# Convolution and channel mix on one core: casting loads, tap matrix from all partitions, a split first group, and the difference on VectorE

## The chip, the cores and the metric

One core of one Trainium2 chip runs the kernel. The metric is the device time of one execution in microseconds (us). A version has four runs in each comparison (the kernel before up to seven); I quote medians and, in brackets, the lowest and highest run.

## The reference

A causal convolution of seven taps runs along the sequence; its taps are a softmax, one set for each of eight heads of 24 channels. An RWKV channel mix follows.

```python
batch, seq, d_model, d_ff = (8, 4160, 192, 1024)      # 8 heads, 7 taps
w = softmax(weight)                                    # per head
x = conv(x, w)                                         # causal, per head
x_prev = shift(x, 1)                                   # one step back, zero first
xk = mu_k * x + (1.0 - mu_k) * x_prev                  # = x_prev + mu_k * (x - x_prev)
xr = mu_r * x + (1.0 - mu_r) * x_prev
k = np.maximum(xk @ w_k, 0.0)
v = k * k @ w_v
r = 1.0 / (1.0 + np.exp(-(xr @ w_r)))
return r * v
```

## The kernel before

Batches go in four pairs. A sequence is cut into blocks of 116 positions with a halo of 6, and nine blocks of both batches make a group. The convolution of one head and one group is one matmul against a banded matrix of that head's taps, the tile `toe`. The result is copied out of PSUM, transposed (`yT`), and mixed: `d = x - x_prev`, then `xk` and `xr`. The main loop has 260 slots, one for 128 of the 1024 hidden features and 512 positions of two batches. In a slot, TensorE makes `k` (4 matmuls), `r` (2) and `v` (8), ScalarE takes the relu, VectorE squares it. Convolutions and transposes of the next group are strewn into the slots.

The order is fixed by hand: each piece is put at a slot of its engine's table, and each engine executes in that order. These are the parts that the change touches:

```python
def cast_x(p, g, s):                       # GpSimd: float32 to bf16, head by head
    ...
    nc.gpsimd.tensor_copy(out=xbs[p, g][:, :, :, s, :],
                          in_=xf.rearrange("p n (h g) -> p h n g", h=H))
...
w_raw = const.tile([H, K], FP32)           # taps on 8 partitions
...                                        # softmax into w_row [8, 244]
w_scr = dram.tile([H, P, W], BF16)         # each row 128 times: 1024 pieces of 488 B
nc.sync.dma_start(out=w_scr, in_=w_row.unsqueeze(1).to_broadcast([H, P, W]))
toe = const.tile([P, H, BLK], BF16)        # read back one element further per partition
nc.sync.dma_start(out=toe, in_=bass.AP(tensor=w_scr.tensor, offset=w_scr.offset + K - 1,
                                       ap=[[W - 1, P], [P * W, H], [1, BLK]]))
...
def diff(p, s):
    ...
    nc.gpsimd.tensor_tensor(out=d[:, :, :L], in0=yT[:, :, c0 : c0 + L],
                            in1=yT[:, :, c0 - 1 : c0 - 1 + L], op=ALU.subtract)
...
nc.vector.tensor_tensor(out=o, in0=k_sb, in1=k_sb, op=ALU.mult)      # the square
```

## Time and profile before

The median is 548.74 us (546.62 to 548.99). I cut the trace by events on TensorE; times count from the start of the span. The span is what the trace shows of a run: 548.0 us of a run of 549.68.

| stretch of the kernel before | us | what rules it |
|---|---|---|
| start to the first k matmul | 44.11 | `toe` lands at 30.4, then convolution, transposes, difference, mixes |
| slots 0 to 15 | 32.44 | ScalarE's copies and the first mixes |
| slot 16 to the last matmul | 467.48 | TensorE, with stalls of 8.7 in all behind VectorE |
| last matmul to the end | 3.94 | last product and store |

To read it: TensorE is the bound wherever its slots repeat to the hundredth. So the question about any other engine is not how busy it is, but how often TensorE waits for it. Two more views put the same into one line each. First, the shares of the chain that ended last, by engine, on the page of the kernel before; then the longest early piece of that chain (start, length, what).

```profile
PE 68%; DVE 17%; issue 7%; DMA 6%; POOL 1%; ACT 1%; SPq 0%; DVEq 0%; POOLq 0%
```

```profile
7.95 14.67 DMA w_scr<-w_row
```

VectorE holds 17% of the chain, which would be 93 us: the share of a chain says who was followed, not what would be saved. One DMA of 488 KB takes 14.67 us of an opening of 44.

### The profile page before, as it was taken

Reading aid. Unit: us, or ns where it says so; the run is one execution under the profiler, and the core shown is the slowest. Engines: PE = TensorE matmul, PEld = TensorE weight load, DVE = VectorE, ACT = ScalarE, POOL = GpSimd, SP = SyncE. Lnnn points to the kernel's source line nnn. Section 1 sums busy time; section 2 is a strip of 40 time slices with the busy share of each in tenths; the row PEclk is TensorE's granted clock in tenths of the full one; section 3 lists DMA queues with packets and bytes.
Section 4 is the critical chain, followed back from the end, with each engine's and each line's share of the span. In section 5 each row is a group of like instructions: output and inputs, shape, how many; then the busy total and the mean of one; then the engine's idle time right before and its main releaser. Section 6 shows DMA issues by size and latency. Waiting matters only on the chain.

```text
span 548.0 us, 10694 instructions
## 1 busy us (share of the span) xinstructions
PE 498.3 (91%) x4248; PEld 359.5 (66%) x4248; DVE 488.6 (89%) x643; ACT 377.9 (69%) x539; POOL 172.7 (32%) x88
## 2 busy tenths in 40 slices
PE   0066889999999999999999999999999999999997
PEld 0032467777777677777777677777777677777776
DVE  1229999999999999999999999999999999989863
ACT  1044876878777686867777686867778587877772
POOL 4135513415034513515034522506134422204000
PEclk9999999999999999999999999999999999999999
DMA  7792013343432334343431334343341341111213
GB/s 199 188 267 65 2 53 114 108 124 108 138 110 60 112 112 123 105 128 109 125 121 49 114 121 123 94 138 109 122 120 49 109 123 61 49 58 45 73 60 95
DMA packets 77438, 57.28 MB, mean 105 GB/s; under 512 B 5778, under 2 KB 77132, under 8 KB 77388
## 3 DMA queue, kind: packets, MB, share of 16 engines
q1 hardware_dynamic: 75132, 54.57, 33.0%
q10 hardware_dynamic: 2256, 2.03, 1.3%
q8 instruction: 33, 0.54, 0.4%
q14 instruction: 17, 0.14, 0.1%
HBM read 30.53 MB, written 26.06 MB: 103 GB/s over the span
## 4 chain that ended last, share of the span: by engine, by line
PE 68%; DVE 17%; issue 7%; DMA 6%; POOL 1%; ACT 1%; SPq 0%; DVEq 0%; POOLq 0%
PE ps_v L390 25%; PE ps_k L314 15%; PE ps_k L310 15%; DVE k L355 7%; DVE xk L277 4%; PE ps_r L371 3%; PE ps_r L372 3%; PE ps_c L198 3%; DMA xf<-in_x_dram 3%; PE ps_t L229 3%; DMA w_scr<-w_row 3%; DVE o_sb L402 2%; DVE xr L277 2%; DVE yT L239 2%; ACT k_sb L341 1%
## 5 line engine op out<-in xcount | busy, mean ns | idle before, releaser
L341 ACT ACTIVATE k_sb<-ps_k 128x1024 bf16<-128x1024 f32 x260 | 265.9, 1023 | 120.7 <-PE ps_k L314 108.7
L355 DVE TENSOR_TENSOR k<-k_sb 128x1024 bf16<-128x1024 bf16 x256 | 254.5, 1005 | 5.6 <-ACT k_sb L341 5.1
L390 PE MATMUL ps_v<-wv,k 128*128 128x192 bf16 x2048 | 211.2, 246 | 3.8 <-DVE o_sb L402 2.7
L390 PEld LDWEIGHTS <-k 128*128 128x128 bf16 x2048 | 173.5, 98 | 39.9 <-issue 5.8
L255 POOL TENSOR_TENSOR d<-yT 128x1536 bf16<-128x1536 bf16 (+1 forms) x36 | 102.2, 2841 | 275.6 <-DVE yT L239 239.0
L310 PE MATMUL ps_k<-xk,wk 128*128 128x512 bf16 x512 | 153.6, 382 | 2.2 <-DVE xk L277 2.2
L314 PE MATMUL ps_k<-xk,wk 128*128 128x512 bf16 x512 | 153.6, 382 | 2.1 <-DVE xk L277 2.1
L314 PEld LDWEIGHTS <-wk 128*128 128x128 bf16 x512 | 50.4, 98 | 63.7 <-issue 4.0
L186 POOL CAST xb<-xf 128x1728 bf16<-128x1728 f32 x32 | 66.2, 2068 | 58.0 <-DMA xf<-in_x_dram 52.3
L402 DVE TENSOR_TENSOR o_sb<-ps_v,r_sb 128x384 f32<-128x384 f32 x132 | 71.8, 544 | 12.2 <-PE ps_v L390 10.3
L277 DVE SCALAR_TENSOR_TENSOR xr<-d,mu,yT 128x1024 bf16<-128x1024 bf16 x64 | 77.0, 1205 | 0.9
L198 PE MATMUL ps_c<-xb,toe 128*116 128x432 bf16 x128 | 46.6, 370 | 31.8 <-DMA toe<-w_scr 30.4
L277 DVE SCALAR_TENSOR_TENSOR xk<-d,mu,yT 128x1024 bf16<-128x1024 bf16 x64 | 69.8, 1092 | 2.9 <-POOL d L255 2.4
L380 ACT ACTIVATE r_sb<-ps_r 128x384 bf16<-128x384 f32 x132 | 65.1, 493 | 10.3 <-PE ps_r L372 8.2
L371 PE MATMUL ps_r<-wr,xr 128*128 128x192 bf16 x256 | 63.0, 246 | 3.3 <-DVE yT L239 3.2
L214 ACT CAST y<-ps_c 116x432 bf16<-116x432 f32 x96 | 44.9, 474 | 30.3 <-PE ps_c L198 30.3
L372 PE MATMUL ps_r<-wr,xr 128*128 128x192 bf16 x256 | 63.0, 246 | 0.0
L310 PEld LDWEIGHTS <-wk 128*128 128x128 bf16 x512 | 46.4, 98 | 4.3 <-issue 4.2
L198 PEld LDWEIGHTS <-toe 128*116 128x116 bf16 x128 | 17.6, 139 | 48.1 <-DMA toe<-w_scr 30.4
L229 PEld LDWEIGHTS <-y 116*128 116x128 bf16 x432 | 30.3, 100 | 23.2 <-issue 5.9
L239 DVE COPY yT<-ps_t 128x696 bf16<-128x696 bf16 (+1 forms) x80 | 38.4, 480 | 7.9 <-PE ps_t L229 7.0
L229 PE MATMUL ps_t<-ident,y 116*128 116x116 bf16 x432 | 36.2, 219 | 2.6 <-DVE yT L239 2.3
(46 smaller groups left out, 121.3 us busy)
## 6 DMA issues: line engine op xcount, KB each, us to landing
out_dram<-o_sb SPq DMA_DIRECT2D x128, 192.0 KB
xf<-in_x_dram SPq DMA_DIRECT2D x23, 864.0 KB
xf<-in_x_dram SPq DMA_DIRECT2D x9, 768.0 KB
stage<-in_moe_w_v_dram ACTq DMA_DIRECT2D x1, 768.0 KB
xf<-in_x_dram SPq DMA_DIRECT2D x8, 84.0 KB
stage<-in_moe_w_k_dram ACTq DMA_DIRECT2D x1, 512.0 KB
stage<-in_moe_w_k_dram ACTq DMA_DIRECT2D x2, 256.0 KB
w_scr<-w_row SPq DMA_DIRECT2D x1, 488.0 KB
```

Source lines behind the costliest of these rows:

```text
L198: nc.tensor.matmul(out=ps[:BLK].rearrange("p n s g -> p (n s g)"), lhsT=toe[:, h, :], rhs=xb[:, h, :, :, :].rearrange("p n s g -> p (n s g)"),
L229: nc.tensor.transpose(out=ps[:, c, i, :], in_=ys[p, g][:BLK, 2 * j + i, c * P : (c + 1) * P], identity=ident[:BLK, :BLK],)
L255: nc.gpsimd.tensor_tensor(out=d[:, :, :L], in0=yT[:, :, c0 : c0 + L], in1=yT[:, :, c0 - 1 : c0 - 1 + L], op=ALU.subtract,)
L277: nc.vector.scalar_tensor_tensor(out=o, in0=d[r0:r1, sl, :L], scalar=mu[r0:r1, i, part : part + 1], in1=yT[r0:r1, sl, c0 : c0 + L], op0=AL ...
L310: nc.tensor.matmul(out=ps[:, i, :], lhsT=wk[:, 0, fs], rhs=xk[:, i, :], start=True, stop=False)
L314: nc.tensor.matmul(out=ps[:, i, :], lhsT=wk[:, 1 + i, fs], rhs=xk[:, 2, :], start=False, stop=True)
L341: nc.scalar.activation(out=k_sb, in_=ps.rearrange("p a b -> p (a b)"), func=AF.Relu)
L355: nc.vector.tensor_tensor(out=o, in0=k_sb, in1=k_sb, op=ALU.mult)
L371: nc.tensor.matmul(out=o, lhsT=hi, rhs=wr[:, 0, :], start=True, stop=False)
L372: nc.tensor.matmul(out=o, lhsT=lo, rhs=wlo, start=False, stop=True)
L390: nc.tensor.matmul(out=o, lhsT=k2[:, f, t * P : (t + 1) * P], rhs=wv[:, f, :], start=(f == 0), stop=(f == NF - 1),)
L402: nc.vector.tensor_tensor(out=o_sb[:, :n, :], in0=v_ps.pop(m)[:, :n, :], in1=r_sbs.pop(m)[:, :n, :], op=ALU.mult)
```

## The change

The intent is to free VectorE of GpSimd's interference and to shorten the opening. x and the weights are loaded by GpSimd's DMAs, which convert to bf16 on the way, so the casts on GpSimd and VectorE and the float32 tiles go. The softmax of the taps is computed on all 128 partitions at once, so the scratch is written in 128 rows of 2 KB. The first group is split into 5 and 4 blocks, and its convolution outputs are copied by ScalarE and VectorE in turn. The difference moves from GpSimd to VectorE. Copies of weight pieces (`fill_tails`) are put on GpSimd at slot 4 in the table of loads. Three smaller moves come with it: `xb` gets three buffers in place of two, the loads of `mu` go from ScalarE's queue to SyncE's, and in the first pair the convolutions of the second and third groups and the differences and mixes that follow them get later slots. The diff, cut to its core:

```diff
-        xf = xfp.tile([P, GB, D], FP32, tag="xf")
-        nc.sync.dma_start(out=xf[:, lo:hi, :], in_=src)
-    def cast_x(p, g, s): ...
+    groups = [... [(0, 5, 0), (5, 4, 1)] + [(g * GB, GB, 2 * g) for g in range(1, NG)] ...]
+        xb = three.tile([P, GB, 2, D], BF16, tag="xb", name="xb")
+            nc.gpsimd.dma_start(out=xb[:, lo:hi, s, :], in_=...x...)      # casts
 ...
-    w_raw = const.tile([H, K], FP32)
+    w_raw = const.tile([P, H, K], FP32)
+    nc.scalar.preload_act_table(AF.Exp)
 ...
-    w_scr = dram.tile([H, P, W], BF16)
-    nc.sync.dma_start(out=w_scr, in_=w_row.unsqueeze(1).to_broadcast([H, P, W]))
+    w_scr = dram.tile([P, H, P], BF16)
+    nc.sync.dma_start(out=w_scr, in_=w_row)
-            ap=[[W - 1, P], [P * W, H], [1, BLK]],
+            ap=[[H * P - 1, P], [P, H], [1, BLK]],
+    nc.scalar.preload_act_table(AF.Sigmoid)
 ...
-        nc.vector.tensor_copy(out=w[:, 0, :], in_=wf[:, 0, :])            # and others
+        nc.gpsimd.dma_start(out=w[:, 0, :], in_=src[0:P, :])              # and others
+    def fill_tails():
+            nc.gpsimd.tensor_copy(out=w[0:LO, 3, :], in_=w[0:LO, 1, :])   # and one more
 ...
-            rhs=xb[:, h, :, :, :].rearrange("p n s g -> p (n s g)"),
+            rhs=xbs[p, g][:, :nb, :, h * G : (h + 1) * G],
 ...
-        nc.gpsimd.tensor_tensor(
+        nc.vector.tensor_tensor(
             out=d[:, :, :L],
 ...
+    at(early, -16, load_rest)
+    at(early, 4, fill_tails)
```

## The prediction

> **What bounds the kernel now.** I read the page's busy row first, then the slices, then the chain of waits in order of time, then the timeline of the first 80 us, then the groups.
>
> ```profile
> PE 498.3 (91%) x4248; PEld 359.5 (66%) x4248; DVE 488.6 (89%) x643; ACT 377.9 (69%) x539; POOL 172.7 (32%) x88
> ...
> PE   0066889999999999999999999999999999999997
> ...
> POOL 4135513415034513515034522506134422204000
> ...
> GB/s 199 188 267 65 2 53 114 108 124 108 138 110 60 112 112 123 105 128 109 125 121 49 114 121 123 94 138 109 122 120 49 109 123 61 49 58 45 73 60 95
> ```
>
> TensorE and VectorE are both near 90%, but they do not bound the same part. One slice is 13.7 us: TensorE does nothing in the first two, is part-filled in the next four, and is full from about 80 us to the end. The chain in that full part consists of TensorE pieces:
>
> ```profile
> 89.30 0.66 PE ps_v L390 x8
> ...
> 91.16 0.66 PE ps_v L390 x8
> ...
> 92.85 0.66 PE ps_v L390 x8
> ...
> 94.54 0.66 PE ps_v L390 x8
> ...
> 96.41 0.66 PE ps_v L390 x8
> ```
>
> The start-to-start distance is one slot of the schedule (there are 260): 1.69 us without extras (92.85 to 94.54), 1.87 with one convolution matmul, 2.00 with six transposes (87.31 to 89.30 in the same list). These repeat exactly wherever TensorE waits for nothing. Sixteen slots hold 8 convolutions and 27 transposes: 8 x 1.87 + 4 x 2.00 + 1.85 + 3 x 1.69 = 29.9 us. A pair of batches (64 such slots and a tail slot of 1.9) should take 121.4 us. The chain shows what it takes:
>
> ```profile
> 122.43 1.56 DVE k L355
> ...
> 246.42 1.56 DVE k L355
> ...
> 370.43 1.56 DVE k L355
> ```
>
> The same event comes back every 124.0 us, so VectorE costs about 2.7 us per pair. Summing actual minus best slot time over all slots from number 16 on, I get 9.2 us of stalls in the whole kernel. The rest is matmul floor. The opening is different:
>
> ```profile
> 7.95 0.84 SPq L116 DMA_DIRECT2D w_scr<-w_row  x1
> ...
> 30.40 0.97 PE L198 MATMUL ps_c<-xb,toe 128*116 128x432 bf16 x2 [30.40 <-DMA toe<-w_scr]
> ...
> 38.67 2.75 POOL L255 TENSOR_TENSOR d<-yT 128x1536 bf16<-128x1536 bf16 x1 [3.93 <-DVE yT L239]
> ...
> 41.45 5.76 DVE L277 SCALAR_TENSOR_TENSOR xk<-d,mu,yT 128x1024 bf16<-128x1024 bf16 x2 [2.42 <-POOL d L255]
> ...
> 44.11 1.01 PE L310 MATMUL ps_k<-xk,wk 128*128 128x512 bf16 x2 [2.19 <-DVE xk L277]
> ```
>
> The first convolution waits 30.4 us for the tap matrix (toe), the first k matmul starts at 44.1, and slot 16 starts at 76.55. The budget is therefore 44.1 (opening) + 32.4 (slots 0 to 15) + 467.5 (slot 16 to the last matmul at 544.0, of which 9.2 are stalls) + 4.0 (last store) = 548.0.
>
> The stalls come from this (the timeline, then the groups):
>
> ```profile
> 61.34 8.17 DVE L355 TENSOR_TENSOR k<-k_sb 128x1024 bf16<-128x1024 bf16 x3
> ```
>
> ```profile
> L355 DVE TENSOR_TENSOR k<-k_sb 128x1024 bf16<-128x1024 bf16 x256 | 254.5, 1005 | 5.6 <-ACT k_sb L341 5.1
> ...
> L255 POOL TENSOR_TENSOR d<-yT 128x1536 bf16<-128x1536 bf16 (+1 forms) x36 | 102.2, 2841 | 275.6 <-DVE yT L239 239.0
> ...
> L186 POOL CAST xb<-xf 128x1728 bf16<-128x1728 f32 x32 | 66.2, 2068 | 58.0 <-DMA xf<-in_x_dram 52.3
> ```
>
> Three squares take 8.17 us exactly while GpSimd runs a difference, a cast and a difference. Undisturbed, one takes 0.68 us (0.60 from start to start); the mean is 1.005.
>
> **What the Trainium skill says.** "SBUF — State Buffer", section "Who interferes with whom": a VectorE instruction with two SBUF inputs contends with a GpSimd instruction that reads SBUF, and the loser blocks for the whole instruction. The trace agrees (0.68 against 2.7 us for those three squares). "VectorE: DVE Perf Modes", section "The perf-mode tier table": tensor_tensor in bf16 reaches 2 elements per cycle. The square agrees: 1024/2/0.96 GHz = 533 ns plus some 150 fixed is 0.68. "Vector Engine (DVE) Microarchitecture Reference", section "Performance modes": 4-byte alignment makes no difference there. This matters as the difference reads one input at an odd column; no instruction of before tests it. "DMA: Bandwidth & Descriptors", section "SWDGE vs HWDGE vs iDMA": a casting DMA can only be issued by GpSimd, whose cores write every descriptor in software. The kernel before has no such DMA, so the trace gives no cost per descriptor. That is the largest unknown.
>
> **The change part by part.**
>
> 1. *GpSimd stops touching SBUF data* (32 casts, 66.2 us, and 36 differences, 102.2 us, go). VectorE gains 256 x (1.005 - 0.68) = 83 us on squares, and on the mixes 32 x (1.365 + 1.360 - 2 x 1.28) + 32 x (1.045 + 0.824 - 2 x 0.75) = 5 + 12 = 17 us. It takes on 36 differences at 1536/2/0.96 + 150 = 0.95 us, so 34 us. Its weight casts (some 5 us, opening only) go. Net busy time about 488 - 83 - 17 + 34 - 5 = 417 us. Per 16 slots, start to start: 16 x 0.60 + 8 x 0.47 + 4 x 0.45 + 0.27 + 4 x (1.19 + 0.66) + 2 x 0.87 = 24.6 us against TensorE's 29.9. VectorE gets slack, but time drops only by the stalls: at most 9.2 us, and I count 7.7 because transposes and mixes still bunch in some slots.
>
> 2. *Tap matrix.* The taps are computed on all partitions with the same small operations. The instruction order shows three table loads in a row before the exponential (the early load of the sigmoid table is placed ahead of it): 0.8 + 3 x 1.28 = 4.7 us, as early as the 5.1 of before, since ScalarE no longer issues DMAs. So w_row is ready near 6 us, as now. The scratch write then goes at once from 128 partitions in 2 KB pieces instead of 1024 pieces of 488 bytes that took 7.95 to 22.7 us: landing near 9. The tap read still has 1024 short pieces (7.3 us before, from 23.05 at the end of its issue to 30.39): landing near 15.
>
> 3. *First group of 5 blocks.* From first convolution to the first k matmul before: 13.7 us. After: convolution pieces of 240 columns evacuated by ScalarE and VectorE in turn, about 3 us; 15 transposes in place of 27, 4.0 x 15/27 = 2.2; difference 0.95 and mixes 1.28 + 0.75 without the contention that made them 2.75 + 5.76. That sums to about 8.5: 15 + 8.5 = 23.5. TensorE's order also has seven convolutions of the second group (4 blocks) ahead of the first k matmul, so they wait for the third batch of DMAs. I take 25, a gain of 19.
>
> 4. *Slots 0 to 15.* ScalarE has a 1.02 evacuation and a 0.51 convolution copy in each of the first ten: 15.3 us. Slots 10 to 15 carry convolutions and transposes together (1.69 + 0.31 + 0.18 = 2.18, three times, then 2.03 and 2 x 1.87): 12.3. With 2.4 for waits, 30.0 against 32.4.
>
> 5. *Casting loads.* Bytes moved are as before, less stage traffic; the stores stay. In the full part loads have two groups (60 us) of lead, so they hide. In the opening, blocks 9 to 17 are needed at slot 1. The bytes ahead of them and theirs (0.98 + 0.79 + 0.79 + 0.15 + 0.79 + 1.77 + 0.5 MB of taps = 5.8) need 22 us at the best rate of the slices, 267 GB/s: ready near 24 if bandwidth alone decides. I leave the 2.4 of part 4 for this.
>
> Sum: 25 + 30 + (467.5 - 7.7) + 4.0 = 518.8, so **519 us**.
>
> **The rivals.** *(a) Descriptor writing bounds the opening.* Some 6,100 row pieces must be described before blocks 9 to 17 are in (1268 + 256 + 1024 + 256 + 1024 + 2304 = 6132). At 2.5 ns each, with 1 us for each of 15 DMAs, that is near 30 us and costs a few us; at 5 ns it is 45 us, TensorE then stalls some 15 us at slot 1, and the time is near 533. At 10 ns it would be near 560, slower than before. For it: eight semaphores for these DMAs, each reused, tie the ninth DMA to the first. Against: the schedule of the first groups was evidently placed late to fit such loads. *(b) VectorE stays the bound.* If the difference runs at one element per cycle it takes 1.75 us; per 16 slots VectorE needs 26.2 of 29.9, so stalls of perhaps 3 to 5 us stay: 522. *(c) Convolution matmuls get slower*, because they now read runs of 24 columns rather than one run of 432. They lie on the bound: 0.18 us x 120; half as slow again is +11 us: 530. Nothing in the profile before shows such a read. *(d) The opening goes better* (first k matmul at 20, no wait at slot 1): 511.
>
> **Range and chances.** All but (a) and (c) keep the time between 511 and 525, and a mild (a) or (c) reaches 534. The verdict line for faster is 548.7 x 0.98 = 537.8, which needs a strong (a), or (a) and (c) together. I give 0.88 to faster, 0.09 to same, 0.03 to slower.
>
> **What would show it.** Right: toe lands near 15; first k matmul near 25; slot 16 near 55; squares at a mean below 0.75 us; the difference on VectorE at 0.95; the chain from 60 us on nearly all TensorE, a pair repeating every 121.5 us. Wrong: a convolution waiting for x in slots 1 to 10 (rival a); slots with a convolution longer than 1.87 (rival c); VectorE pieces in the chain of the full part (rival b); a load landing late after 100 us.

## More of the kernel before

The stalls are the sum, over all slots from 16 on, of a slot's time less the shortest of its kind (plain, with a convolution, with transposes). This count gives 8.7 us; the prediction has 9.2.

## The result

The changed kernel took 523.67 us (521.39 to 525.93) against 548.74. All outputs are right. The ratio is 0.955, with a 95% interval of 0.950 to 0.961. Ratios here are the mean time of one kernel's runs over that of the other's in the same rounds, so not quite the ratio of the medians. The predicted 519 is 4.7 us too low; the range of 509 to 534 held it. The profiled run took 521.39 us, one of the short ones.

Same cuts as before:

| stretch | before | after | change | predicted |
|---|---|---|---|---|
| start to the first k matmul | 44.11 | 26.25 | -17.9 | -19 |
| slots 0 to 15 | 32.44 | 30.01 | -2.4 | -2.4 |
| slot 16 to the last matmul | 467.48 | 459.07 | -8.4 | -7.7 |
| last matmul to the end | 3.94 | 4.34 | +0.4 | 0 |

The page of the changed kernel (busy row; slices of 13.0 us, in tenths; shares of the chain):

```profile
PE 492.5 (95%) x4256; PEld 360.1 (69%) x4256; DVE 425.3 (82%) x676; ACT 380.0 (73%) x545; POOL 51.9 (10%) x74
...
PE   0597999999999999999999999999999999999996
...
POOL 9532100001020000101002010100100000000000
...
PE 92%; DMA 3%; DVE 2%; ACT 2%; issue 0%; DVEq 0%; SPq 0%
```

VectorE fell from 89% to 82% and GpSimd's data work nearly vanished. The chain went from 68% to 92% TensorE: from slot 16 on, TensorE waits for almost nothing (stalls of 0.3 us in all by the same count, against 8.7; the view of TensorE's waits lists none between 57 and 512 us). The chain in order of time, one event per pair of batches, shows the period:

```profile
124.45 0.66 PE ps_v L388 x8
...
245.65 0.66 PE ps_v L388 x8
...
366.86 0.66 PE ps_v L388 x8
```

It is 121.2 us in place of 124.0. The groups of the page give the reason (mean ns of one instruction behind the busy us; L87 is the casting load, for which the time is that of issuing it):

```profile
L353 DVE TENSOR_TENSOR k<-k_sb 128x1024 bf16<-128x1024 bf16 x256 | 175.0, 684 | 24.2 <-ACT k_sb L339 22.6
...
L87 POOL DMA_DIRECT2D xb<-in_x_dram x34 | 32.2, 950 | 247.3 <-PE ps_c L193 218.4
...
L253 DVE TENSOR_TENSOR d<-yT 128x1536 bf16<-128x1536 bf16 (+1 forms) x36 | 32.0, 889 | 0.1
```

The mean square is 684 ns, the undisturbed value, and the difference on VectorE costs 32 us in all (889 ns is the mean with the four short ones of the tails). The opening, from the timeline:

```profile
6.13 0.34 SPq L137 DMA_DIRECT2D w_scr<-w_row  x1
...
12.15 0.39 SPq L139 DMA_DIRECT2D toe<-w_scr  x1
...
16.40 0.65 PE L193 MATMUL ps_c<-xb,toe 128*116 128x240 bf16 x2 [16.40 <-DMA toe<-w_scr]
...
22.34 1.06 POOL L176 COPY wk<-wk 64x1024 bf16<-64x1024 bf16 x1
22.81 1.41 DVE L253 TENSOR_TENSOR d<-yT 128x1536 bf16<-128x1536 bf16 x1
...
26.25 1.01 PE L308 MATMUL ps_k<-xk,wk 128*128 128x512 bf16 x2 [1.37 <-DVE xk L275]
```

The taps are ready at 6.1. The scratch is not down until 12.1 and `toe` lands at 16.4, where the first convolution starts. The first difference and the first mix lie beside copies on GpSimd (`fill_tails`) and take longer than later ones: 1.41 against some 0.95 for the difference.

### The profile page after: what moved, and what is told of

Its sections match the earlier page's. It is cut to its first block, busy times and chain, and to the rows that moved or that the text cites. A ratio compares the mean times of both kernels' runs of the same rounds, so it can differ in the third digit from the quotient of the medians.

```text
span 519.7 us, 10640 instructions
## 1 busy us (share of the span) xinstructions
PE 492.5 (95%) x4256; PEld 360.1 (69%) x4256; DVE 425.3 (82%) x676; ACT 380.0 (73%) x545; POOL 51.9 (10%) x74
## 4 chain that ended last, share of the span: by engine, by line
PE 92%; DMA 3%; DVE 2%; ACT 2%; issue 0%; DVEq 0%; SPq 0%
PE ps_v L388 33%; PE ps_k L308 21%; PE ps_k L312 21%; PE ps_c L193 4%; PE ps_t L226 4%; PE ps_r L370 4%; PE ps_r L369 4%; ACT k_sb L339 1%; DMA w_scr<-w_row 1%; DMA toe<-w_scr 1%; DVE yT L237 1%; DMA w_raw<-in_weight_dram 1%; DVE xk L275 1%; DVE d L253 0%; PE ps_k L326 0%
## 5 line engine op out<-in xcount | busy, mean ns | idle before, releaser
L353 DVE TENSOR_TENSOR k<-k_sb 128x1024 bf16<-128x1024 bf16 x256 | 175.0, 684 | 24.2 <-ACT k_sb L339 22.6
L275 DVE SCALAR_TENSOR_TENSOR xk<-d,mu,yT 128x1024 bf16<-128x1024 bf16 x64 | 65.5, 1024 | 0.6
L193 PE MATMUL ps_c<-xb,toe 128*116 128x432 bf16 (+2 forms) x136 | 46.6, 346 | 20.0 <-DMA toe<-w_scr 16.4
L275 DVE SCALAR_TENSOR_TENSOR xr<-d,mu,yT 128x1024 bf16<-128x1024 bf16 x64 | 64.7, 1015 | 0.9
L210 ACT CAST y<-ps_c 116x432 bf16<-116x432 f32 (+4 forms) x99 | 45.5, 460 | 16.3 <-PE ps_c L193 16.0
L87 POOL DMA_DIRECT2D xb<-in_x_dram x34 | 32.2, 950 | 247.3 <-PE ps_c L193 218.4
L193 PEld LDWEIGHTS <-toe 128*116 128x116 bf16 x136 | 18.6, 138 | 32.4 <-DMA toe<-w_scr 16.4
L253 DVE TENSOR_TENSOR d<-yT 128x1536 bf16<-128x1536 bf16 (+1 forms) x36 | 32.0, 889 | 0.1
```

What stands on the lines that cost most here:

```text
L193: nc.tensor.matmul(out=ps[:BLK, :nb], lhsT=toe[:, h, :], rhs=xbs[p, g][:, :nb, :, h * G : (h + 1) * G], start=True, stop=True,)
L275: nc.vector.scalar_tensor_tensor(out=o, in0=d[r0:r1, sl, :L], scalar=mu[r0:r1, i, part : part + 1], in1=yT[r0:r1, sl, c0 : c0 + L], op0=AL ...
```

## The experiments

Each version was run in rounds with the kernel before on the same chip. The parts were undone singly in the changed kernel, then put singly into the kernel before; then three things that the trace of the changed kernel had shown to cost time were taken away.

### r1_after_again: the changed kernel once more

No edit; a control.

> The changed kernel again, unaltered, as the control of this call and to see what separates its runs of 521 to 522 us from those of 525 to 526. If the spread lies in the opening (DMA landings), slot 16 starts anywhere from 56 to 60 us and the full part stays at 459.1 us from slot 16 to the last matmul. If it lies in the full part, that stretch varies instead. Time 521 to 526.

523.0 us (521.28 to 525.35), ratio 0.953 (0.950 to 0.956). Over both calls, the eight runs lie at 521.3 to 522.2 (four) and 524.0 to 525.9 (four). The profiled run is one of the long ones (525.35), so the two traces can be compared. The DMA view of this long run, with the issue-to-landing time at the end of each line:

```profile
w_scr<-w_row SPq DMA_DIRECT2D x1, 256.0 KB, 5.9
toe<-w_scr SPq DMA_DIRECT2D x1, 232.0 KB, 7.1
```

`toe` takes 7.1 us here and 4.2 in the short run; the first k matmul follows at 29.05 in place of 26.25, slots 1 and 2 take 1.1 us more, and from slot 3 on the two are alike. So the two clusters are decided in the first 36 us, and in these two traces what splits them first is the landing of `toe`.

The 1.1 us have another cause. These are slot 2's first two k matmuls, in the short run, then in the long one (timeline):

```profile
30.36 0.59 PE L308 MATMUL ps_k<-xk,wk 128*128 128x512 bf16 x2
```

```profile
33.52 1.06 PE L308 MATMUL ps_k<-xk,wk 128*128 128x512 bf16 x2
```

TensorE starts at half rate (1.06 us for two, against 0.59 later) and, by the clock record of the trace, changes to full rate at 29.96 in the short run, 3.7 us after the first k matmul, but at 35.07 in the long one, 6.0 after. The Trainium skill explains that, in "TensorE: Matmul & The Clock Gate", section "Part 1: The HAM clock gate": a window of 3413 ns runs free of the program, and the clock is raised after a busy one. The records agree: the time at full clock is 143.0 such windows in both runs, and 145.0 in the kernel before. That the place of a run's start in the window moved the time by about a microsecond fits this, with nothing changed in the kernel; no run varied that place, so it is argued and not shown. It matters for every comparison of first slots below: a step that comes later after the first k matmul makes them longer.

### e1_diff_pool: the difference back on GpSimd

```diff
-        nc.vector.tensor_tensor(
+        nc.gpsimd.tensor_tensor(
             out=d[:, :, :L],
```

> The changed kernel with only the difference put back on GpSimd (same places in the order). Theory (the stalls of the full part were GpSimd reading SBUF beside VectorE's two-input instructions, and the difference was the larger share, 102 of 168 us): squares rise from a mean of 684 ns to about 850, some 1 us of TensorE stalls per pair comes back, the opening gets 2 to 3 us longer because the difference takes 2.75 in place of 1.41 us there; together 3 to 7 us slower. Rival (the casts were what made the stalls, the move of the difference is neutral): within 1.5 us of the control, no stalls from slot 16 on.

531.32 us (530.83 to 531.86), 8.3 more than the control's median, above the 3 to 7 expected. But its `toe` lands at 19.2, as in the control's trace, and against that long run it is 6.1 us (span 529.69 against 523.62). The squares, and the two that took longest (group, then timeline):

```profile
L353 DVE TENSOR_TENSOR k<-k_sb 128x1024 bf16<-128x1024 bf16 x256 | 245.3, 966 | 12.1 <-ACT k_sb L339 11.3
```

```profile
109.16 6.96 DVE L353 TENSOR_TENSOR k<-k_sb 128x1024 bf16<-128x1024 bf16 x2
110.77 2.02 POOL L87 DMA_DIRECT2D xb<-in_x_dram  x2
...
112.80 2.77 POOL L253 TENSOR_TENSOR d<-yT 128x1536 bf16<-128x1536 bf16 x1
```

The mean square is back at 966 ns with no cast left in the kernel: the difference alone does nearly all of the damage to the squares, though not to the time (see e4). The 216 squares that no difference overlaps take 682 ns; the 44 that one overlaps take 2334 on average. The period of a pair is 122.1 instead of 121.2, and with the first pair the stretch from slot 16 on is 2.8 us longer; slots 0 to 15 grow by 2.5 and the opening by 0.8. One of the two squares above lasted 4.83 us, from 111.30 to 116.13, beside a DMA issue and then the whole next difference. It is no single case: three such squares of 4.83 to 4.84 us and three of 3.78 to 3.80 began 1.5 and 0.5 us before the difference, while GpSimd by the trace only issued DMAs. Why they were held from there stays open.

### e4_before_diff_dve: the kernel before, with only the difference moved

```diff
-        nc.gpsimd.tensor_tensor(
+        nc.vector.tensor_tensor(
 ...
-            at(pool, n0 - 7, diff, p, s)
+            at(dve, n0 - 7, diff, p, s)
```

> The kernel before with only the difference moved to VectorE; casts of x stay on GpSimd. Theory (the difference on GpSimd made most of the stalls and some 4 us of the opening): the pair of batches repeats every 121.2 to 121.5 us in place of 124.0, the stretch from slot 16 to the last matmul falls from 467.5 to about 460, the opening gets 2 to 5 us shorter as the difference takes 1 in place of 2.75 us and the mixes behind it meet one cast less; total 537 to 541. Rival (the 66 us of casts are enough for the stalls): the pair stays above 122.5 us, total 543 or more.

538.06 us (536.72 to 539.46) against 549.11: ratio 0.981 (0.978 to 0.984), so about 11 us; at the threshold of 2% the verdict is unclear. The squares:

```profile
L355 DVE TENSOR_TENSOR k<-k_sb 128x1024 bf16<-128x1024 bf16 x256 | 184.9, 725 | 15.2 <-ACT k_sb L341 14.0
```

The casts still run on GpSimd (32, 59.8 us), yet the mean is only 725 ns: 25 squares that overlap a cast take 1116 ns on average, the other 235 take 682. So the two GpSimd operations, which the prediction took as one part, are unequal for the squares: 2334 ns beside a difference (e1) against 1116 beside a cast, and in the kernel before 1735 against 1365 where only one of the two overlaps. The traces show what the hold is made of. One cast and one square here (timeline):

```profile
432.29 2.45 POOL L186 CAST xb<-xf 128x1728 bf16<-128x1728 f32 x1 [11.14 <-DMA xf<-in_x_dram]
433.17 2.11 DVE L355 TENSOR_TENSOR k<-k_sb 128x1024 bf16<-128x1024 bf16 x1
```

The square ends at 435.28, 0.54 us after the cast. All 90 squares of over 0.83 us in the traces of e1, this run and the kernel before end 0.54 to 0.56 us after a difference or a cast. So a held square waits for the end of the GpSimd instruction, whichever it is, and the two differ in how much there is to wait for: a full difference lasts 2.74 to 3.77 us in e1, a cast 1.62 to 2.55 here. Of the 44 squares beside a difference 31 were held, of the 25 beside a cast 12. From slot 16 on this run needs 462.09 us (some 460 was expected), against 467.48 before and 459.07 after: taking the difference away brings 5.4 of the 8.4. But that is not its share: with only the casts left, the stretch is 3.0 longer than after the change; with only the differences left (e1) 2.8; with both 8.4. For TensorE the two cost about the same singly, and together more than their sum. A VectorE that has room for one of them and not for both would give this; no run tested that reason.

### e3_old_taps: the old tap path in the changed kernel

```diff
-    w_raw = const.tile([P, H, K], FP32)
+    w_raw = const.tile([H, K], FP32)          # softmax on 8 partitions
 ...
-    w_scr = dram.tile([P, H, P], BF16)
-    nc.sync.dma_start(out=w_scr, in_=w_row)
+    w_scr = dram.tile([H, P, W], BF16)
+    nc.sync.dma_start(out=w_scr, in_=w_row.unsqueeze(1).to_broadcast([H, P, W]))
```

> The changed kernel with the taps' path of before: softmax on 8 partitions, scratch written as 1024 pieces of 488 bytes from 8 partitions. Theory (the tap matrix sets the start of the first convolution): the scratch write takes 10 to 15 us in place of 5.9, toe lands at 21 to 26 in place of 16.4, the first k matmul follows it by the same 10 us, and the total rises by 4 to 9 us. Rival (x or the weights arrive late anyway, the taps only look like the wait): total within 1.5 us of the control.

534.29 us (533.21 to 535.12), 11.3 more than the control's median, where 4 to 9 was expected. Trace against trace it is 7.9 more than the control's long run (span 531.52 against 523.62) and 11.8 more than the short one. The scratch is issued at 5.63, the read of `toe` only at 20.73, and the first convolution starts at 28.72, as against 19.20 in the control's trace. From slot 16 on nothing differs (459.12).

### e9_before_new_taps: the kernel before, with only the new tap path

The edit is the reverse of the last one, in the kernel before.

> The kernel before with only the taps' path exchanged (softmax on all partitions, scratch in 2 KB pieces). Theory (the many short pieces from 8 partitions made the scratch write slow): the scratch write takes 5 to 8 us in place of 14.7, toe lands at 20 to 24 in place of 30.4, the first k matmul starts 4 to 9 us earlier, bounded by x and the weights' casts that end at 31 us; total 540 to 545. Rival (the staged weight loads beside it made it slow): scratch still 11 us or more, total above 546.

542.24 us (541.17 to 542.96) against 549.11: ratio 0.988 (0.986 to 0.991), 6.9 us. The first convolution starts at 23.99 in place of 30.40. The scratch is issued later here (9.57) than in the changed kernel (6.13) and takes 7.9 us, against 14.67 in the kernel before with the same weight loads beside it, so the new form of the write is what shortened it. So the tap path has more to give when the rest of the opening is rebuilt too: 11.3 when undone, 6.9 when done alone.

### e10_before_diff_taps: both of these in the kernel before

```diff
-        nc.gpsimd.tensor_tensor(
+        nc.vector.tensor_tensor(
 ...
-    w_raw = const.tile([H, K], FP32)
+    w_raw = const.tile([P, H, K], FP32)       # and the rest of the new tap path
```

> The kernel before with both the difference on VectorE and the new taps' path, loads and casts as before. Theory (the two parts are independent: one shortens the wait for toe, the other the way from toe to the first k matmul and the stalls of the full part): 549 - 11.0 - 6.9 = 531.2, so 530 to 533; toe's landing as in the run with the taps alone (24.0), slot 16 to the last matmul as in the run with the difference alone (462.1). What is then left to the changed kernel's 523 is the share of the casting loads and the split group, 7 to 10 us. Rival (toe is no longer what the opening waits for once the difference is gone, x or weights are): the taps add less than 4 us, total above 534.

532.31 us (531.46 to 532.90) against 548.97: 16.7 us. The singles sum to 11.0 + 6.9 = 17.9, so they nearly add. `toe` is there at 23.90 and the first k matmul comes at 35.87. The trace has lost some matmul records; by ScalarE's relu of slot 16, which it has, the stretch from there to the last matmul is 460.14 (before 466.42, after 458.01). The rest of the way to the changed kernel, 532.3 to some 523.3, is 9 us. It belongs to the casting loads, the split group, the shared copies and the three smaller moves together; the share of the casting weight loads alone was not measured.

### e2_one_group: the first group of nine blocks whole

```diff
-        else [(0, 5, 0), (5, 4, 1)] + [(g * GB, GB, 2 * g) for g in range(1, NG)]
+        else [(g * GB, GB, 2 * g) for g in range(NG)]
```

> The changed kernel with the first group of nine blocks left whole. Theory (the split shortens the path from the tap matrix to the first k matmul): first k matmul 2.8 us later, at about 29.0 (1.2 more for wider convolution pieces, 1.6 for 12 more transposes); slots 0 to 15 shorter by 1 to 2 us because the second half's convolutions and transposes are not in them; total 1 to 2 us slower. Rival (the split costs as much as it gives): same within 0.5 us.

525.65 us (525.53 to 526.43), 2.6 more than the control's median. But all four runs lie at or just above the long runs of the changed kernel. In its trace the first convolution, which waits for `toe`, starts at 19.07, much as in the long run of the control (19.20). From there to the first k matmul this version takes 11.61 us and the control 9.85; slots 0 to 15 then take 29.77 and 31.14. The spans are 523.86 and 523.62, so at the same landing of `toe` the split brings 0.4 us against this trace. But part of the 31.14 is the clock: full rate comes 6.0 us after the first k matmul in the control and 4.0 here. In the short run it comes after 3.7, slots 0 to 15 take 30.01, and against that run, the landing of `toe` taken off, the split brings 1.5 us (1.8 in the opening, less 0.2 in the slots, into which the second part's convolutions move). So it is worth between 0.4 and 1.5 us; single traces cannot say more. What the split may bring beyond that is that `toe` lands early in half of the runs, which no run of this version showed; four runs are few for that.

### e6_table: no early load of the sigmoid table

The timeline of the changed kernel shows ScalarE's table loads, three in a row and one later:

```profile
0.82 1.28 ACT L102 ACT_TABLE_LOAD   x1 [0.82 <-PEq L485]
...
2.11 1.28 ACT L147 ACT_TABLE_LOAD   x1
...
3.39 1.28 ACT L126 ACT_TABLE_LOAD   x1
...
41.95 1.28 ACT L378 ACT_TABLE_LOAD   x1
```

The preload of the sigmoid (L147) came ahead of the exponential (L126), which had to load its own table again, and at 41.95 the sigmoid's is loaded once more, just when its first result is needed. The edit puts a real sigmoid of one column after the exponential, so the order is fixed by data:

```diff
-    nc.scalar.preload_act_table(AF.Sigmoid)
+    w_sig = const.tile([P, 1], FP32)
+    nc.scalar.activation(out=w_sig, in_=w_exp[:, 0, 0:1], func=AF.Sigmoid)
```

> The changed kernel with the preload of the sigmoid table replaced by a one-column sigmoid of the exponentials, so that the table comes after the exponential and is not loaded again in slot 10. Theory (the 1.28 us load in slot 10 holds the k evacuation and so TensorE): slot 10 takes about 2.2 in place of 2.95 us, the total falls by 0.7 to 1.3 us. Rival (the load hides under another wait of slots 10 to 13): no change. The tap matrix is not earlier, since the taps themselves land at 4.6 us, after the three table loads of before were nearly done. The spread of the control (toe at 16.4 or 19.2) is larger than this effect, so the slots decide, not the total.

521.70 us (520.00 to 522.87), ratio 0.951 against 0.953 to 0.955 for the changed kernel. There are two loads, at 0.81 and 5.50, and none at the first sigmoid. Slot 10 takes 2.18 us in place of 2.95, and no other slot from 3 to 15 changes. So the preload costs 0.8 us in the place it stands; the intervals of the two overlap, and it is the trace that settles it. In this trace the first convolution starts at 17.95, between the 16.40 and 19.20 of the changed kernel, so the landing of `toe` takes more than two values.

### e8_held_loads: GpSimd's loads wait for the tap matrix

Added to e6_table: GpSimd copies one column of `w_row` ahead of the second group's loads and one column of `toe` ahead of the weights and the third group, so the first are issued after the taps are ready, and the others after `toe` has landed.

```diff
+    hold = const.tile([P, 2], BF16)
+    def wait_pool(i, src):
+        nc.gpsimd.tensor_copy(out=hold[:, i : i + 1], in_=src)
-    load_w(wk, moe_w_k)
-    at(early, -16, load_rest)
+    at(early, -25, wait_pool, 0, w_row[:, 0, 0:1])
+    at(early, -20, wait_pool, 1, toe[:, 0, 0:1])
+    at(early, -19, load_w, wk, moe_w_k)
+    at(early, -12, load_rest)
```

> As e6, and GpSimd holds back casting loads while the taps' two DMAs are under way: a one-column copy of w_row makes it wait before the loads of the second group, a one-column copy of toe before wk, the third group, wr and wv. Theory (the taps' scratch write of 5.9 us and the tap read of 4.2 or 7.1 us are slow only because the casting loads share the DMA engines with them): scratch lands at 9 to 10.5 in place of 12, toe at 12.5 to 14.5 in place of 16.4 to 19.2, and its landing no longer jumps between runs; the first k matmul starts at 22.5 to 24.5; total 517 to 520. Rival (the two DMAs are bound by their own latency and piece count): toe at 16 or later and total as the control. Risk: wk or the third group's x come too late, then TensorE waits for wk at slot 0 or for xb at slot 1.

517.11 us (516.69 to 517.46), ratio 0.943 (0.941 to 0.945): 4.6 below e6_table, and no two clusters. The DMA view:

```profile
w_scr<-w_row SPq DMA_DIRECT2D x1, 256.0 KB, 2.8
...
toe<-w_scr SPq DMA_DIRECT2D x1, 232.0 KB, 3.7
```

The scratch takes 2.8 us in place of 5.9, `toe` 3.7 in place of 4.2 or 7.1; the first convolution starts at 12.90 and the first k matmul at 21.65. The bytes are the same. In the traces of the next two runs, which hold the loads back too, the scratch takes 3.4 and 2.9, `toe` 3.3 and 4.0. So about half of the scratch's 5.9 us in the changed kernel was the cost of standing beside the casting loads, and so was `toe`'s 7.1 in the long run; the 4.2 of the short run is hardly above what it takes without them. The packet records of the changed kernel agree: the scratch was issued at 6.13, its 2 KB packets first move at 9.53, and between lie packets of the `wk` load.

### e8_again: the same once more

No edit against e8_held_loads; a control on another chip.

> The kernel with the sigmoid table loaded once and the casting loads held back, again, on the chip of this call, as the control of the next run: 516.5 to 517.6 us, toe at 12.5 to 13.2.

517.36 us (517.21 to 517.76), ratio 0.943 (0.941 to 0.945).

### e11_held_tails_late: the weight copies moved to slot 24

```diff
-    at(early, 4, fill_tails)
+    at(early, 24, fill_tails)
```

against e8_held_loads.

> As e8, with the GpSimd copies and memsets that fill the tail weights moved from slot 4 to slot 24 of the order. Theory (these copies read SBUF while VectorE mixes and squares of the first slots run, and block them: a square took 1.52 us, the two mixes 2.73 in place of 2.03): the first two mixes take 2.0 us, no square over 0.7 us in the first slots, the total falls by 0.5 to 1.5 us to about 516. Rival (the first slots wait for ScalarE and x anyway): no change.

516.63 us (516.57 to 516.81), ratio 0.942 (0.940 to 0.944), 0.7 below its control. The two mixes for the first k matmuls, in e8_held_loads and then here:

```profile
20.31 2.73 DVE L279 SCALAR_TENSOR_TENSOR xk<-d,mu,yT 128x1024 bf16<-128x1024 bf16 x2
```

```profile
20.65 1.95 DVE L279 SCALAR_TENSOR_TENSOR xk<-d,mu,yT 128x1024 bf16<-128x1024 bf16 x2
```

Of the two, the first mix takes 1.28 us in both, the second 1.53 and then 0.75. By the trace the copies of e8_held_loads start at 23.80, after this second mix, beside which GpSimd only issues DMAs; as in e1, a hold comes before GpSimd's own data work, and why stays open. Beside the copies themselves lie the next mix and a square (1.52 us each). Against e8_again the first k matmul is no earlier (8.75 us after the first convolution in both). The gain is in the first slots: ScalarE's relu of slot 16 comes 30.55 us after the first k matmul in place of 31.28. The expectation that no square would exceed 0.7 us failed: GpSimd reaches the copies at 26.31 already, and squares and a difference lie beside them there (the longest square 1.34 us). This version is faster than both kernels: 5.8% below the kernel before, and some 1.2 to 1.4% below the changed one (0.942 over 0.953 to 0.955).

## Why the prediction was right, and what it mis-sized

**The bound.** Right. It read TensorE as the bound and VectorE's 89% as nearly harmless: of 488.6 us busy, only the stalls were to be had. VectorE lost 63 us (488.6 to 425.3) and the full stretch 8.4.

**Part 1, GpSimd off SBUF.** Right in mechanism; the squares went to 684 ns. The gain was put at 7.7 and measured 8.4. The count of stalls was 0.5 too high (9.2, where the count by kinds of slot gives 8.7 before and 0.3 after), and nearly all of them went: the reserve for slots in which work bunches was not needed. The floor of 121.4 for a pair has one convolution twice, since the tail slot's 1.9 holds it already; 121.2 is what was measured. Two points were missing. The cast and the difference do not add: in the stretch from slot 16 on, the casts alone cost 3.0 us (e4), the differences alone 2.8 (e1), and both 8.4, although the squares suffer far more from the differences. And GpSimd did not leave SBUF altogether: the copies of `fill_tails` are new data work in the opening. Beside them the first difference took 0.5 and the first mix 0.7 us longer in the trace; e11 shows 0.7 us of the time for their place once `toe` is early, where they lie beside later instructions.

**Part 2, the tap matrix.** The taps at 6.1 were right, as was the order of the three table loads. The step that failed is "landing near 9": the scratch took 5.9 us and landed at 12.1. Its size was taken as if it had the DMA engines to itself; e8_held_loads, in which it nearly has, shows 2.8 and a landing near 9.2, so the 9 was right for that case alone. `toe` was put at 6 us on from the scratch, whereas it took 4.2 or 7.1. The sum, "near 15", became 16.4 or 19.2. Of the two traces' spans, 519.7 and 523.6, against the sum of 518.8, this excess of 1.4 or 4.2 us and the 1.1 of the long run are the larger part; the shorter full stretch and smaller terms take 0.5 off again. The rest of the way to the measured times is the 1.7 us by which a run is longer than its span: the prediction added up a span and took it for the time. The prediction had counted bytes ahead of blocks 9 to 17, but not those that run beside the scratch.

**Part 3, the first group.** From the first convolution to the first k matmul the working gave 8.5 (its terms sum to 8.2) and took 10; it measured 9.85, both times. The terms: convolutions 4.1 (predicted 3), transposes 2.3 (2.2), difference 1.41 (0.95), and 1.95 for the first mix, which alone the first k matmul waits for (1.28; the 0.75 for the second was not on the path). The seven convolutions of the second part did not wait for a load. What it did not part is the split's own share: the opening gains 1.8 by it, the first slots give some of that back, and at the same landing of `toe` 0.4 to 1.5 us are left (e2).

**Part 4, slots 0 to 15.** The 30.0 was met to the hundredth in the short run, partly by luck. Slots 10, 11 and 13 took 2.9 rather than 2.2; one of the three was the table load (e6), and in the other two the waits are convolutions that wait for VectorE's copy of `yT`, which frees a PSUM buffer. In the long run the stretch was 31.1, by TensorE's later step to full clock, of which the prediction had no term. It bears on the gain of 2.4 too: in the kernel before the step comes 8.1 us after the first k matmul (at 52.19), in the short run 3.7.

**Part 5, casting loads.** Right as far as their own use goes: no convolution waits for x, in slot 1 or later. What they did to the tap matrix is the miss of part 2. The two loads of blocks 9 to 17 were down at 20.8 and 23.2, where the working had 24.

**The rivals.** (a) Descriptor writing is not the bound: a casting load of 1152 rows takes about 1.0 us to issue, one of 128 rows 0.56, so about 0.4 ns a row on top of 0.5 us, far from the 5 or 10 ns of the rival. But the rival touched the right part: the casting loads did cost time in the opening, by what they move and not by what is written to start them. (b) is refuted: the full difference takes 0.95 us, at its odd column too, so it runs at two elements per cycle. (c) is refuted: slots with one convolution take 1.87 us, as before, though the operand now comes in runs of 24 columns. (d) comes nearest to what e8 reached (first k matmul at 21.65), not the change as made.

**What stays open.** Why `toe` lands at 16.4 in some runs and at 19.2 in others of the same program; why some VectorE instructions were held while GpSimd by the trace only issued DMAs (six squares in e1, a mix in e8_held_loads); what the split alone is worth between 0.4 and 1.5 us; and how the last 9 us divide among the casting x loads, the casting weight loads, the split, the shared copies and the smaller moves.

## What to carry to other kernels

Take the value of relieving a busy engine from the waits that the bounding engine has for it, summed over the stretch where they occur (here 8.7 us, with VectorE busy for 488), and take the opening by itself, transfer by transfer. A transfer on the critical path must be sized beside what else moves in the same microseconds; if the other loads can wait, make them wait by a data dependence, which was worth more here (4.6 us) than splitting the first group. When work leaves an engine for the sake of another, look for new work that the same change puts there.

## What the Trainium skill lacked or had wrong

- "DMA: Bandwidth & Descriptors", section "SWDGE vs HWDGE vs iDMA", says that hardware sets up faster than software but gives no cost for a row. The runs: 0.56 us to issue 128 rows, 0.77 to 0.90 for 512, 0.95 to 1.02 for 1152.
- The same section tells that an engine takes its queues in turn. It has no number for what a small critical transfer loses beside casting loads: 256 KB took 5.9 us beside them and 2.8 to 3.4 with them held back; 232 KB took 4.2 or 7.1, and 3.3 to 4.0. No page gives the longer packet of a casting load: 51 to 54 ns for a row of 768 B read and 384 B written, where a plain row of 768 B takes 36 to 42 (both from the packet records).
- "SBUF — State Buffer", section "Who interferes with whom", calls the port pair that VectorE and GpSimd share an exclusive lock. This holds: squares beside neither took 682 ns, and each of the 90 held ones ended 0.54 to 0.56 us after a GpSimd instruction, cast or difference alike. It infers that descriptor writing leaves such an instruction alone, and the changed kernel agrees: 19 squares and 15 mixes ran beside the issue of a casting load, the longest square 693 ns. It does not cover what e1 and e8_held_loads show: squares and a mix held while GpSimd by the trace issued DMAs ahead of data work of its own (squares up to 4.84 us).
- "ScalarE: Activation LUTs", section "What ACT_TABLE_LOAD costs", has 1283 ns for the load, and the traces 1.28 us. The drain of about 1380 ns that it adds for every switch is not there between loads in a row (0.82, 2.11 and 3.39: one after the other without a gap), nor at the load between two results (the relu before it ends at 41.93, the load runs from 41.95, the sigmoid starts at 43.25).
